# Strided attention tiles in pairs, block 0's logits on VectorE, and another order of the work ahead of the FFN

## The chip, the cores and the metric

The kernel runs on one core of a Trainium2 chip. The metric is the device time of one execution, in microseconds (us).

## What is computed

Attention, a dense FFN and a gated expert layer, one after the other, over 4 x 576 = 2304 tokens of width 512:

```python
mask_local = (rel >= 0) & (rel < 32)
mask_strided = (rel >= 0) & (pos[None, :] % 32 == pos[:, None] % 32)
masks = np.stack([mask_local if h < 4 else mask_strided for h in range(8)])
attn = softmax(where(masks, q @ k.T / 8, -1e9))        # 4 batches, 8 heads of width 64
x = attn @ v                                           # [2304, 512]
...
r = np.maximum(x @ w_in, 0)                            # w_in [512, 2048]
x = (s * r * r + b) @ w_out                            # w_out [2048, 512]
...
skip = x @ w_skip > 0                                  # only these tokens are computed
e = argmax(x @ w_gate)                                 # one of 8 experts
out = x + softmax(x @ w_gate)[e] * (relu(x @ w1[e]) @ w2[e])
```

## The kernel before, in words

**Attention.** The eight heads of a batch are taken as four pairs of heads: two local ones (`loc`, window 32) and two strided ones. The 16 pairs n (batch n // 4) are worked through in the order local, strided, local, strided of each batch, and each is cut into three units g. A local unit has three tiles of 128 queries by 96 keys. A strided unit has 4, 4 and 3 tiles of 108 queries (54 of each head) by 54 keys, since after sorting the positions by their remainder only keys of the same three remainders meet. `add_unit` makes the tasks of a unit: `scores` (PE), `masked` and `top` (DVE), `bias`, `exps` (ACT), `recip`, `norm` (DVE), `turned` (PE: one transpose for each tile, into the PSUM bank `pt`), `moved` (ACT: `pt` to `pts` in SBUF), `mixed` (PE: the products with V, for each tile one matmul for each head, side by side in two column halves of the array), and the puts, `hi` (ACT) and `lo` (DVE), which split the result into two fp32r parts in `xb`, the FFN's input. For pairs from `PAIRED` on the two heads' scores too are computed side by side in column halves of the array; below it they come from one matmul over both heads. For pairs below `BYPE` the mask is added by PE.

**FFN.** There are 6 blocks of 384 tokens and 16 chunks `fc` of the hidden width, so 96 steps i. A step is `mm1` (12 matmuls, L1150), the elementwise `relu`, `square`, `g_hi`, `g_lo`, and `mm2` (9 matmuls, L1193) into three PSUM banks. The first 8 steps are half of block 0, then comes all of block 1, then block 0's second half, then blocks 2 to 5. Block 0 and 1 need batches 0 and 1, the later blocks batches 2 and 3, whose attention units stand between the FFN's steps. The weights come as fp32 and are split into two fp32r parts on DVE and ACT (the last step of a split is L580 on DVE); the eighth pair of weights is wanted at about 100 us, the last one at about 140 us.

**Routing and experts.** When a block is done its logits are computed, on PE (`logits_pe`: four times three transposes, L652, and two matmuls, L666, then a small turn, L681) or on DVE (`logits_v`: 27 dot products, L703, over gate rows that a DMA spreads over all partitions). `DOTS` names the blocks that take DVE. `route_rank` follows, on PE. The experts' phase runs at the end, in its own loops.

**What sets the order.** A planner (`plan.add`) holds every task with its engine costs, its priority, what it waits for and which buffers it takes. It fixes the program order of each engine ahead of time from these costs and from tables of offsets (`UNIT_AT`, `LOAD_AT`, `CHUNK_AT`); on the chip each engine then runs its own list in order and waits on semaphores. DMAs are issued from SP's list.

Of the kernel before, what the change touches and what calls it, by code (L numbers as in the profile page):

```python
# [21 lines left out]
BLK = 384  # L22
# [9 lines left out]
BYPE, SQ_A = 8, 8  # L32
# [4 lines left out]
LATE, LEAD = 3.0, 0  # L37


PAIRED, AHEAD = 8, 2  # L40
TURN_AT, PACE = (26.0, 44.0), 1.4
DOTS = (2, 3)
# [12 lines left out]
    1.1, 1.9, -0.6, -2.9, -0.4, 1.2, -0.7, 12.3, 11.2, -14.2, -8.5, 1.8,  # L55
# [6 lines left out]
]  # L62

SEM, PELAT, DMA, FLEX = 0.34, 0.22, 2.0, 0.4
# [125 lines left out]
def kernel(  # L190
# [53 lines left out]
    sx = [pm.tile([128, 512], F32, name=f"sx{i}") for i in range(2)]  # L244
# [42 lines left out]
    vb = wp.tile([96, 2 * 11 * D], F32, name="vl")  # L287
# [4 lines left out]
    x_tasks = {k: [] for k in range(NBLK)}  # L292
# [14 lines left out]
    def place(n, g):  # L307
        return wanted(n, g) if n < PAIRED else in_turn[3 * (n - PAIRED) + g]

    def add_pair(n):  # L310
# [22 lines left out]
        def load_v(e):  # L333
            if n in V_ROOM:
                for h in range(2):
                    vt[h] = make(vbuf[h], [nk, nt_all, D], F32)
                    SY.dma_start(vt[h][:], vd[:, h])
            else:
                v = vb[0:nk, 0:2 * nt_all * D].rearrange("p (h t d) -> p h t d", h=2, t=nt_all)
                SY.dma_start(v, vd)  # L340
                vt[:] = [v[:, 0], v[:, 1]]
# [17 lines left out]
        if n in V_ROOM:  # L359
            vbuf = [Buf([r]) for r in V_ROOM[n]]  # L360
        lv = plan.add(c_dma(4 * nk * 2 * nt_all * D), load_v, p0 - 3.5 + LOAD_AT[n], after=() if n in V_ROOM else o_tasks.get(n - 1, ()), take=vbuf, lat=DMA)
        s_tasks[n], o_tasks[n] = [], []
        for g in range(3):
            prio = place(n, g)
            add_unit(n, b, hp, g, loc, qk, vt, vbuf, qbuf, nq, nk, by_pe, prio, lq[min(g, 1)], lv)

    def add_unit(n, b, hp, g, loc, qk, vt, vbuf, qbuf, nq, nk, by_pe, prio, lq, lv):
        ts = [3 * g + t for t in range(3)] if loc else [4 * g + t for t in range((4, 4, 3)[g])]
# [7 lines left out]
        xo_b = Buf(["xo0", "xo1"] + ["x2p1", "x2p2"] * first)  # L376
# [50 lines left out]
        def norm(e):  # L427
            ENG[e].tensor_tensor(m3(d["s"]), m3(d["s"]), d["sm"][0:np_, 4:4 + nt, None].to_broadcast([np_, nt, nk]), op=ALU.mult)

        def turned(e):  # L430
            d["pt"] = pt = make(pt_b, [128, 512], F32)
            for i in range(nt):
                PE.transpose(pt[0:nk, i * np_:(i + 1) * np_], m3(d["s"])[:, i, :], ident[0:np_, 0:np_])  # L433

        def moved(e):
            d["pts"] = make(pts_b, [128, 432], F32)
            dst, src = d["pts"][0:nk, 0:nt * nq], d["pt"][0:nk, 0:nt * np_]
            if np_ > nq:
                dst = dst.rearrange("p (t h c) -> p t h c", t=nt, h=2)
                lo = src.rearrange("p (t c) -> p t c", t=nt)  # L440
                src = bass.AP(lo.tensor, lo.offset, [lo.ap[0], lo.ap[1], [64, 2], [1, nq // 2]])
            copy(e, dst, src)

        def cols(i, t):
            lo = 18 if not loc and t == 10 else 0
            return lo, nq // 2 - lo

        def mixed(e):
            d["xo"] = xo = make(xo_b, [128, 512], F32)
            c = 0  # L450
# [14 lines left out]
        if halved and len(mixes) >= AHEAD:  # L465
            t = plan.extend(mixes[-AHEAD], {"PE": nt * (0.16 if loc else 0.12)}, scores, after=[lq], take=[sc_b], use=qbuf)
# [4 lines left out]
        if halved and len(mixes) >= AHEAD:  # L471
            gates.append((turns[-AHEAD], b, prio))
        if not by_pe:
            t = plan.add(c_v(w), masked, prio, after=[t, consts], take=[s_b], use=[sc_b])
        t = plan.add(c_v(w), top, prio, after=[t], take=[sm_b], use=[sc_b] if by_pe else [s_b])
        t = plan.add(c_v(8), bias, prio, after=[t], use=[sm_b])
        t = plan.add({"A": nt * (0.25 + nk / 1400)}, exps, prio, after=[t], take=[s_b] if by_pe else [], use=[sm_b] + ([sc_b] if by_pe else [s_b]))
# [13 lines left out]
        if loc:  # L491
            k_, o = divmod(b * S + 192 * g, BLK)
            parts.append((k_, 192, lambda w_, k_=k_, o=o: xb[k_ % 3][:, w_, hp, o:o + 192], lambda xo: xo[:, 0:192]))
        else:
            r0, nr = 12 * g, n_out // 18
            j0 = 0
            while j0 < 18:
                k_, o = divmod(b * S + 32 * j0, BLK)
                nj = min(18 - j0, (BLK - o) // 32)
                parts.append((k_, nr * nj,  # L500
                              lambda w_, k_=k_, o=o, nj=nj: xb[k_ % 3][:, w_, hp, o:o + 32 * nj].rearrange("p (j r) -> p r j", r=32)[:, r0:r0 + nr, :],
                              lambda xo, j0=j0, nj=nj: xo[:, 0:18 * nr].rearrange("p (r j) -> p r j", j=18)[:, :, j0:j0 + nj]))
# [16 lines left out]
    for n in range(len(pairs)):  # L519
# [863 lines left out]
```

## Time and profile before

| | |
|---|---|
| median of three runs | 743.59 us (741.44 to 744.49) |
| the profiled execution | 741.3 us, its span 739.5 us |
| PE busy | 723.3 us, 98% of the span |
| DVE / ACT / POOL busy | 400.1 / 294.1 / 62.7 us |
| mean granted TensorE clock | 0.992 |
| DMA | 98 GB/s over the span |

The span is the time between the first and the last instruction of the trace; what lies around it (1.8 us) is in the execution's time alone. Matmuls are pipelined and overlap in the trace: what a group of them costs is read from the start of one group to the start of the next, not from its length.

### The profile page before, as it was taken

How to read it: one execution, taken by the hardware profiler on the slowest of the kernel's cores; microseconds unless marked ns; L12 is line 12 of the kernel's file. 1: busy time of each engine (PE TensorE's matmuls, PEld its weight loads, DVE VectorE, ACT ScalarE, POOL GpSimd, SP SyncE). 2: the span in 40 equal slices, each digit the busy share in tenths (PEclk: the TensorE clock that was granted, in tenths of full speed). 3: DMA queues.
4: the chain of work that ended last, by engine and by line, in shares of the span. 5: the costliest groups of instructions: out<-in, count | busy, mean ns of one | idle time of the engine just before them, and what ended most of it. 6: DMA issues, size and time to landing. Idle time of an engine off the chain costs nothing.

```text
span 739.5 us, 12203 instructions
## 1 busy us (share of the span) xinstructions
PE 723.3 (98%) x4513; PEld 623.0 (84%) x4517; DVE 400.1 (54%) x1092; ACT 294.1 (40%) x819; POOL 62.7 (8%) x67
## 2 busy tenths in 40 slices
PE   8899999999999999999999999999999999999996
PEld 6788788998888888888899988898787888888894
DVE  4889999826554744688646664654442222312221
ACT  4777776524353554544422224443211312203120
POOL 0000000000010100000100012110023212122131
PEclk9989999999999999999999999999999999999998
DMA  9875655202240222331021104420203701112021
GB/s 291 279 249 174 205 185 183 85 1 86 92 151 1 74 82 71 132 117 47 30 95 47 45 14 156 154 64 0 86 9 110 291 29 43 44 43 71 30 76 45
DMA packets 26895, 73.74 MB, mean 100 GB/s; under 512 B 5557, under 2 KB 5813, under 8 KB 26821
## 3 DMA queue, kind: packets, MB, share of 16 engines
q1 hardware_dynamic: 22741, 61.56, 25.3%
q0 software_dynamic: 3936, 11.03, 4.7%
q8 instruction: 41, 0.67, 0.4%
q10 hardware_dynamic: 144, 0.22, 0.1%
q14 instruction: 33, 0.27, 0.1%
HBM read 57.67 MB, written 15.13 MB: 98 GB/s over the span
## 4 chain that ended last, share of the span: by engine, by line
PE 81%; issue 5%; DVE 5%; DMA 4%; ACT 3%; POOL 1%; SPq 0%; POOLq 0%; ACTq 0%; DVEq 0%
PE h L1150 25%; PE x2p L1193 24%; PE h L920 10%; PE x2p L933 8%; DMA out<-row,ids 4%; PE sx L455 2%; PE pt L433 2%; PE sx L399 2%; PE sx L401 1%; PE h L1303 1%; DVE xb L462 1%; DMA wo<-in_w_out 1%; PE x2p L985 1%; PE sx L666 1%; PE pt L652 1%
## 5 line engine op out<-in xcount | busy, mean ns | idle before, releaser
L1150 PE MATMUL h<-xb,wi 128*128 128x384 f32 x1152 | 222.8, 342 | 0.5 <-ACT r L1155 0.5
L1150 PEld LDWEIGHTS h<-xb,wi 128*128 128x128 f32 x1152 | 203.4, 188 | 7.8 <-ACT r L1155 0.9
L1193 PE MATMUL x2p<-wo,gh 128*128 128x512 f32 x564 | 194.6, 399 | 0.0
L1193 PEld LDWEIGHTS x2p<-wo,gh 128*128 128x128 f32 x564 | 105.9, 188 | 21.1
L1193 PE MATMUL x2p<-wo,gl 128*128 128x512 f32 x282 | 110.8, 393 | 0.0
L920 PE MATMUL h<-xb,wi 128*128 128x512 f32 (+1 forms) x480 | 103.3, 374 | 1.4 <-DVE row L937 1.0
L920 PEld LDWEIGHTS h<-xb,wi 128*128 128x128 f32 x480 | 83.5, 188 | 19.4 <-issue 1.6
L933 PE MATMUL x2p<-wi,wo 128*128 128x512 f32 x432 | 99.4, 390 | 0.0
L1155 ACT ACTIVATE r<-h 128x384 f32<-128x384 f32 x96 | 47.0, 490 | 128.6 <-PE h L1150 112.6
L1158 DVE SCALAR_TENSOR_TENSOR r<-r,sbc 128x384 f32<-128x384 f32 x88 | 54.3, 617 | 76.6 <-ACT r L1155 76.4
L933 PEld LDWEIGHTS x2p<-wi,wo 128*128 128x128 f32 x432 | 80.7, 188 | 16.6
L923 ACT ACTIVATE wo<-h 128x512 fp32r<-128x512 f32 (+1 forms) x40 | 22.2, 555 | 142.8 <-PE h L920 136.8
L1162 ACT ACTIVATE gh<-r,sbc 128x384 fp32r<-128x384 f32 x88 | 54.3, 617 | 53.0 <-DVE r L1158 30.1
L1167 DVE SCALAR_TENSOR_TENSOR gl<-r,sbc,gh 128x384 fp32r<-128x384 f32 x88 | 54.3, 617 | 33.1 <-ACT gh L1162 27.1
L924 DVE SCALAR_TENSOR_TENSOR wo<-h,wo 128x512 fp32r<-128x512 f32 (+1 forms) x40 | 25.5, 638 | 75.4 <-ACT wo L923 74.4
L822 POOL DMA_INDIRECT lst<-pay,ii x18 | 18.4, 1022 | 496.3 <-DVE ii L816 474.5
L1193 PEld LDWEIGHTS x2p<-wo,gl 128*128 128x128 f32 x282 | 53.1, 188 | 8.0
L937 DVE SCALAR_TENSOR_TENSOR row<-x2p,ids,xb 128x512 f32<-128x512 f32 x14 | 10.5, 750 | 61.7 <-PE x2p L933 61.7
L703 DVE SCALAR_TENSOR_TENSOR junk<-row,lo 128x512 int8<-128x512 f32 x54 | 37.2, 690 | 6.2 <-DMA lo<-wgt 5.3
L462 DVE TENSOR_TENSOR xb<-sx,xb 128x192 fp32r<-128x192 f32 (+4 forms) x64 | 19.6, 333 | 7.8 <-ACT xb L277 5.1
L277 ACT CAST xb<-sx 128x192 fp32r<-128x192 f32 (+4 forms) x56 | 15.9, 337 | 18.0 <-PE sx L401 6.6
L938 POOL DMA_INDIRECT out<-row,ids x14 | 14.0, 997 | 106.1 <-DVE row L937 92.7
(481 smaller groups left out, 769.1 us busy)
## 6 DMA issues: line engine op xcount, KB each, us to landing
wo<-in_w SPq DMA_DIRECT2D x16, 512.0 KB
wo<-in_w_out SPq DMA_DIRECT2D x12, 512.0 KB
x2d<-row SPq DMA_DIRECT2D x21, 256.0 KB
qks<-in_qkstr SPq DMA_DIRECT2D x6, 882.0 KB
wo<-in_w_in SPq DMA_DIRECT2D x10, 512.0 KB
out<-row SPq DMA_DIRECT2D x18, 256.0 KB
lo<-wgt SPq DMA_DIRECT2D x18, 256.0 KB
qkl<-in_qkloc SPq DMA_DIRECT2D x5, 864.0 KB
```

What stands on the lines that cost most here:

```text
L462: V.tensor_tensor(dst(1), src(d["xo"]), dst(0).bitcast(F32), op=ALU.subtract)
L703: V.scalar_tensor_tensor(junk[:], d["rows"][t][:], 1.0, wd["w"][:], op0=ALU.mult, op1=ALU.mult, accum_out=d["lg"][:, t, x:x + 1])
L920: PE.matmul(p[:, 0:N], W[f][:, w, k * 128:(k + 1) * 128], x[:, k, 0:N], start=n == 0, stop=n == 11)
L923: A.activation(h[:, 0, 0:N], p[:, 0:N], AF.Relu)
L924: V.scalar_tensor_tensor(h[:, 1, 0:N], p[:, 0:N], 0.0, h[:, 0, 0:N].bitcast(F32), op0=ALU.max, op1=ALU.subtract)
L933: PE.matmul(y[:], K["h"][f][:, g, c], W[NFE + f][:, w, :], start=n == 0, stop=n == 3 * NFE - 1)
L1150: PE.matmul(p[:, 0:BLK], win_t[fc][:, w, k * 128:(k + 1) * 128], x[:, k, :], start=n == 0, stop=n == 11)
L1155: A.activation(d["r"][:], d["p"][:, 0:BLK], AF.Relu)
L1158: V.scalar_tensor_tensor(d["r"][:], d["r"][:], sbc[:, 0:1], d["r"][:], op0=ALU.mult, op1=ALU.mult)
L1162: A.activation(gh[:], d["r"][:], AF.Identity, bias=sbc[:, 1:2])
L1167: V.scalar_tensor_tensor(gl[:], d["r"][:], sbc[:, 1:2], gt[i][0][:].bitcast(F32), op0=ALU.add, op1=ALU.subtract)
L1193: PE.matmul(x2p[t][:], g[:, c], wout_t[fc][:, w, :], start=begins and n == 0, stop=ends and n == 2)
```

## The change

1. *Strided tiles in pairs.* A strided unit's tiles are now t and t + 6 beside t + 1 and t + 7. The two tiles of a pair stand 64 columns apart in the tile `s_`, so that one transpose of 118 columns turns both: the first to partitions 0 to 53, the second to 64 to 117. The ten columns between them are zeroed by a GpSimd memset for each unit (`gap`). `moved` copies half the columns. V is loaded in two halves, tiles 0 to 5 on partitions 0 to 53 and 6 to 10 on 64 to 117 (two DMAs instead of one). `mixed` then has four matmuls for a pair of tiles, one in each quarter of the array, and the two row halves write to two PSUM banks: `xo0` and `xo1` in batches 0 and 1, `xo` and the end of `pt` in batches 2 and 3. The puts of strided units become twice as many and half as wide, except in batch 1 (g below 2), where one instruction reads both banks.
2. *`PAIRED` 8 to 4.* Batch 1's scores are computed in column halves too; their mask is still added by PE, now by two matmuls.
3. *`EARLY` = 4.* The first four `mm1` are cut into 9 matmuls that need the first three pairs of heads (`x_first`) and 3 matmuls (`mm1_last`) that need the fourth.
4. *`DOTS` with block 0.* Its logits go from PE to DVE.
5. *Order.* Batch 1's units have a hand-written order (`SECOND`), the tables and a few planner constants change, and the squares of steps 8 and 9 go the way of the first eight (`SQ_A` 8 to 10).

```diff
-PAIRED, AHEAD = 8, 2
+LATE, LEAD = 3.3, 0
+
+
+PAIRED, AHEAD = 4, 2
...
+SECOND, SECOND_AT = (0, 4, 3, 5, 11, 6, 9, 10, 1, 2, 7, 8), (-5.11, 0.99)
...
-DOTS = (2, 3)
+DOTS = (0, 2, 3)
+EARLY = 4
...
         def load_v(e):
-            if n in V_ROOM:
+            if not loc:
+                v = make(vbuf[0], [128, 2, 6, D], F32)[:] if n in V_ROOM else vb[:, 0:12 * D].rearrange("p (h t d) -> p h t d", h=2, t=6)
+                vt[:] = [v[:, h] for h in range(2)]
+                for r, t in ((0, slice(0, 6)), (1, slice(6, 11))):
+                    SY.dma_start(v[64 * r:64 * r + nk, :, 0:t.stop - t.start].rearrange("p h t d -> p h (t d)"), vd[:, :, t].rearrange("p h t d -> p h (t d)"))
...
+        ts = [3 * g + t for t in range(3)] if loc else [2 * g + t for t in ((0, 6, 1, 7), (0, 6, 1, 7), (0, 6, 1))[g]]
...
+        xo_b = [Buf(["xo0", "xo1"] + ["x2p1", "x2p2"] * first)]
+        if not loc:
+            xo_b = [Buf([f"xo{r}"] + [f"x2p{r + 1}"] * first) for r in range(2)] if b < 2 else [*xo_b, pt_b]
...
+            if by_pe and halved:
+                for h in range(2):
+                    PE.matmul(m3(sc)[64 * h:64 * h + nq // 2], idb[0:np_, 64 * h:64 * h + nq // 2], mask, start=True, stop=False)
+            elif by_pe:
                 PE.matmul(m3(sc), idb[0:nq, 0:nq], mask, start=True, stop=False)
...
+        def gap(e):
+            d["s"] = make(s_b, [128, 288], F32)
+            G.memset(d["s"][0:np_, 0:256].rearrange("p (t k) -> p t k", k=128)[:, :, 54:64 if nt == 4 else 118], 0.0)
...
         def turned(e):
             d["pt"] = pt = make(pt_b, [128, 512], F32)
-            for i in range(nt):
-                PE.transpose(pt[0:nk, i * np_:(i + 1) * np_], m3(d["s"])[:, i, :], ident[0:np_, 0:np_])
+            if loc:
+                for i in range(nt):
+                    PE.transpose(pt[0:nk, i * nq:(i + 1) * nq], s3(d["s"])[:, i, :], ident)
+            else:
+                for i in range(0, nt, 2):
+                    PE.transpose(pt[0:118, i // 2 * np_:(i // 2 + 1) * np_], d["s"][0:np_, 64 * i:64 * i + 118], ident[0:np_, 0:np_])
 
         def moved(e):
-            d["pts"] = make(pts_b, [128, 432], F32)
-            dst, src = d["pts"][0:nk, 0:nt * nq], d["pt"][0:nk, 0:nt * np_]
-            if np_ > nq:
-                dst = dst.rearrange("p (t h c) -> p t h c", t=nt, h=2)
-                lo = src.rearrange("p (t c) -> p t c", t=nt)
-                src = bass.AP(lo.tensor, lo.offset, [lo.ap[0], lo.ap[1], [64, 2], [1, nq // 2]])
-            copy(e, dst, src)
-
-        def cols(i, t):
-            lo = 18 if not loc and t == 10 else 0
-            return lo, nq // 2 - lo
+            d["pts"] = make(pts_b, [128, 384], F32)
+            k, c = (nk, nt * nq) if loc else (118, np2 * np_)
+            copy(e, d["pts"][0:k, 0:c], d["pt"][0:k, 0:c])
...
+            d["xo"] = [d["pt"][:, 384:512] if x is pt_b else make(x, [128, 512], F32) for x in xo_b]
...
+                r, j = i % 2, i // 2
+                lo = 18 if t == 10 else 0
...
+                    c = j * np_ + h * (np_ - 54)
+                    PE.matmul(d["xo"][r][64 * h:64 * h + 64, 54 * j:54 * (j + 1) - lo], vt[h][64 * r:64 * r + 54, 2 * g + j, :], d["pts"][64 * r:64 * r + 54, c + lo:c + 54], start=True, stop=True)
...
+            both = b == 1 and g < 2
+            for r in range(1 if both else 2):
+                r0, nr = 30 if g == 2 and r else 18 * r + 6 * g, 2 if g == 2 and r else 6
...
+    def products(p, X, L, fc, ks, begins, ends):
+        todo = [(k, w, x) for k in ks for w, x in ((0, X), (0, L), (1, X))]
+        for n, (k, w, x) in enumerate(todo):
+            PE.matmul(p[:, 0:BLK], win_t[fc][:, w, k * 128:(k + 1) * 128], x[:, k, :], start=begins and n == 0, stop=ends and n == len(todo) - 1)
...
+            products(p, X, L, fc, HPS[0:3] if i < EARLY else range(4), True, i >= EARLY)
+
+        def mm1_last(e, d=d, blk=blk, fc=fc):
+            products(d["p"], xb[blk % 3][:, 0], xb[blk % 3][:, 1], fc, HPS[3:], False, True)
...
+        if i < EARLY:
+            m1 = plan.add(c_pe(BLK, 9, False), mm1, i - 3000, after=x_first + w_done["i", fc], take=[h_b], use=[wbuf["i", fc]])
+            m1 = plan.add(c_pe(BLK, 3, False), mm1_last, i - 3000, after=[m1, *after, *x_tasks[0]], use=[h_b, wbuf["i", fc]])
```

In the rows below, `x12` counts equal instructions behind one another, `im` is the identity, `s__` a unit's probabilities, `qks`, `qkl` and `vl` the loaded queries, keys and values, `wi_` and `wo_` weights or what shares their buffers.

**A strided unit among the FFN's steps.** PE's list in block 4's attention, before: a transpose for each of four tiles, an `mm1`, the eight products in one bank, the next unit's scores, its transposes.

```order
L433 MATMUL pt<-im,s__3489 54x118 x4
L1150 MATMUL h<-xb_88,wi_876 128x384 x12
L455 MATMUL sx_91<-pts,vl 64x54 x8
L399 MATMUL sx_92<-qks 54x54 x6
L433 MATMUL pt<-im,s__3584 54x118 x4
```

After, at block 2's units: two transposes of 118 rows, an `mm1`, the products in fours, each four with two in bank `sx` and two in bank `pt`.

```order
L461 MATMUL pt<-im,s__2515 118x118 x2
L1181 MATMUL h<-xb_90,wi_696 128x384 x12
L480 MATMUL sx<-pts,vl 64x54 x2
L480 MATMUL pt<-pts,vl 64x54 x2
L480 MATMUL sx<-pts,vl 64x54 x2
L480 MATMUL pt<-pts,vl 64x54 x2
L416 MATMUL sx<-qks 54x54 x6
```

What moved: two of four transposes are gone, and neighbouring products now lie in different row halves; their number is the same.

**The first FFN steps.** PE's list before, around the first `mm1` (L1150; L1146 are matmuls that only keep the clock up): the 12 matmuls stand together, behind the last unit of block 0.

```order
L1146 LDWEIGHTS im
L1146 MATMUL h<-im 128x512
L1150 MATMUL h<-xb_88,wi_530 128x384 x12
L455 MATMUL sx_92<-pts,wi_596 64x64
L455 MATMUL sx_92<-pts,wo_598 64x64
L455 MATMUL sx_92<-pts,wi_596 64x64
L455 MATMUL sx_92<-pts,wo_598 64x64
L455 MATMUL sx_92<-pts,wi_596 64x64
L455 MATMUL sx_92<-pts,wo_598 64x64
L433 MATMUL pt<-im,s__641 96x128 x3
```

After, at the second `mm1` (the nine matmuls with `wi_518` of the first stand 19 rows further up):

```order
L1195 MATMUL h<-im 128x512
L1181 MATMUL h<-xb_88,wi_696 128x384 x9
L1181 MATMUL h<-xb_88,wi_518 128x384 x3
L458 MATMUL pt<-im,s__707 96x128 x3
L473 MATMUL x2p_756<-pts,wi_245 64x64
L473 MATMUL x2p_756<-pts,wo_247 64x64
L473 MATMUL x2p_756<-pts,wi_245 64x64
L473 MATMUL x2p_756<-pts,wo_247 64x64
L473 MATMUL x2p_756<-pts,wi_245 64x64
L473 MATMUL x2p_756<-pts,wo_247 64x64
L1181 MATMUL h<-xb_88,wi_696 128x384 x3
```

What moved: nine matmuls each of the first two steps stand ahead of the last strided unit's puts, and three of each behind them, with a local unit of batch 1 between.

**Block 0's logits.** PE's list before, one of four rounds of three transposes and two matmuls between the parts of the FFN's steps.

```order
L666 MATMUL sx_91<-pts,wgr 18x384
L666 MATMUL sx_91<-lo,wgr 9x384
L652 MATMUL pt<-im,row 128x128 x3
L1150 MATMUL h<-xb_90,wi_1012 128x384 x12
L666 MATMUL sx_91<-pts,wgr 18x384
```

After, PE's list has no such rows for block 0; the work is in DVE's list, between the FFN's elementwise steps (L1206 `square`, L1215 `g_lo`) and the next units' (L427 `masked`, L431 `top`, L434 `bias`, L486 put).

```order
L1206 SCALAR_TENSOR_TENSOR r<-r,sbc 128x384
L1215 SCALAR_TENSOR_TENSOR gl<-r,sbc,gh 128x384
L1206 SCALAR_TENSOR_TENSOR r<-r,sbc 128x384
L427 TENSOR_TENSOR s__2974<-sx,im 128x288
L486 TENSOR_TENSOR xb_88<-sx,xb_88 128x192
L431 TENSOR_REDUCE sm<-s__2974 128x3
L747 SCALAR_TENSOR_TENSOR junk,lg<-row,lo 128x512
L1215 SCALAR_TENSOR_TENSOR gl<-r,sbc,gh 128x384
L747 SCALAR_TENSOR_TENSOR junk,lg<-row,lo 128x512 x2
L434 TENSOR_SCALAR sm<-sm 128x3
```

What moved: 27 dot products (L747) stand in DVE's list across twelve steps, and block 0's `route_rank` on PE, which waits for the last of them, stands some ten steps later than before.

## Rows read from the trace of the kernel before

**Rows 1.** The page's chain that ended last, shares of the span by engine.

```profile
PE 81%; issue 5%; DVE 5%; DMA 4%; ACT 3%; POOL 1%; SPq 0%; POOLq 0%; ACTq 0%; DVEq 0%
```

**Rows 2.** Stretches: busy PE, PEld, DVE, ACT, POOL (instructions), clock, DMA share, GB/s.

```profile
24.00:42.00 18.00, 15.65 (x177) 13.66 (x176) 15.13 (x58) 12.79 (x57) 0.00 (x0) 0.82 0.74 232
42.00:101.00 59.00, 56.61 (x463) 48.57 (x465) 54.55 (x154) 46.29 (x155) 0.00 (x0) 1.00 0.63 200
101.00:140.00 39.00, 38.51 (x194) 34.73 (x193) 38.43 (x72) 24.98 (x45) 0.00 (x0) 1.00 0.57 182
140.00:515.00 375.00, 374.96 (x2448) 330.88 (x2447) 218.48 (x624) 154.37 (x421) 20.99 (x20) 1.00 0.22 72
```

**Rows 3.** Timeline of PE: start, length, line, operation; strided units of batches 2 and 3.

```profile
235.09 0.57 PE L433 MATMUL pt<-im,s__2547 118*54 118x118 f32 x4
235.42 0.48 PE L1193 MATMUL x2p<-wo,gh 128*128 128x512 f32 x1
...
237.95 0.67 PE L455 MATMUL sx<-pts,vl 54*64 54x54 f32 x16
238.56 0.39 PE L399 MATMUL sx<-qkl 128*64 128x96 f32 x4
...
241.74 0.54 PE L455 MATMUL sx<-pts,vl 54*64 54x54 f32 x12
242.22 0.47 PE L399 MATMUL sx<-qkl 128*64 128x96 f32 x6
```

**Rows 4.** Timeline of PE, single matmuls of two strided units of batch 1.

```profile
72.01 0.22 PE L455 MATMUL sx<-pts,wi 54*64 54x54 f32 x1
72.02 0.22 PE L455 MATMUL sx<-pts,wo 54*64 54x54 f32 x1
72.07 0.22 PE L455 MATMUL sx<-pts,wi 54*64 54x54 f32 x1
...
87.67 0.20 PE L455 MATMUL sx<-pts,wi 54*64 54x36 f32 x1
87.67 0.20 PE L455 MATMUL sx<-pts,wo 54*64 54x36 f32 x1
87.70 0.22 PE L455 MATMUL sx<-pts,wi 54*64 54x36 f32 x1
```

**Rows 5.** Timeline of PE, logits of block 0.

```profile
222.23 0.34 PE L666 MATMUL sx<-pts,wgr 128*18 128x384 f32 x1
...
222.58 0.49 PE L652 MATMUL pt<-im,row 128*128 128x128 f32 x3
222.83 0.42 PE L1150 MATMUL h<-xb,wi 128*128 128x384 f32 x1
...
237.67 0.36 PE L681 MATMUL pt<-im,lo 18*128 18x18 f32 x3
```

**Rows 6.** Dots on DVE: the page's row of L703, and the stretch of block 2's.

```profile
L703 DVE SCALAR_TENSOR_TENSOR junk<-row,lo 128x512 int8<-128x512 f32 x54 | 37.2, 690 | 6.2 <-DMA lo<-wgt 5.3
...
246.00:300.00 54.00, 53.96 (x448) 46.53 (x448) 28.18 (x88) 27.66 (x99) 2.63 (x3) 1.00 0.21 70
300.00:352.00 52.00, 52.00 (x420) 45.45 (x418) 41.26 (x124) 24.74 (x79) 0.00 (x0) 1.00 0.34 106
```

**Rows 7.** Waits of DVE from 20 to 101: us, times, longest.

```profile
DVE xb L462 <- ACT xb L277: 3.8, 5, 1.3
```

**Rows 8.** The put on DVE by width, busy and mean ns.

```profile
L462 DVE TENSOR_TENSOR xb<-sx,xb 128x144 fp32r<-128x144 f32 x15 | 6.2, 412 | 3.7 <-ACT xb L277 2.3 <-ACT s__1134 L419 1.3
...
L462 DVE TENSOR_TENSOR xb<-sx,xb 128x72 fp32r<-128x72 f32 x15 | 4.2, 283 | 1.5 <-ACT s__886 L419 0.8 <-ACT xb L277 0.6
```

**Rows 9.** Timelines around 100: DVE's end of a weight, PE's start with it.

```profile
99.44 0.69 DVE L580 TENSOR_TENSOR wo<-row,wo 128x512 fp32r<-128x512 f32 x1
...
101.46 0.40 PE L1193 MATMUL x2p<-wo,gh 128*128 128x512 f32 x1
```

**Rows 10.** The chain of waits, 36 to 45: start, length.

```profile
42.31 2.15 PE h L1150 x12
```

More of the change, by code (lines that the diff above doesn't have):

```diff
@@ L54 @@
 LOAD_AT = [
[L55 removed]
+    2.1, 2.4, -0.9, -2.7, -1.0, 1.2, -2.6, 12.3, -14.2, 6.8, -8.5, 1.8,
     1.6, -9.2, 4.2, 0.7,
@@ L241 @@
     xb = [wp.tile([128, 2, 4, BLK], F32R, name=f"xb{i}") for i in range(3)]
-    sx = [pm.tile([128, 512], F32, name=f"sx{i}") for i in range(2)]
+    sxs = pm.tile([128, 2, 512], F32, name="sx")
+    sx = [sxs[:, i] for i in range(2)]
     halves = {f"sc{i}": sx[i][:, 0:SCW] for i in range(2)} | {f"xo{i}": sx[i][:, SCW:512] for i in range(2)}
@@ L286 @@
     qks = wp.tile([128, S + 2 * 11 * 54], F32, name="qks")
-    vb = wp.tile([96, 2 * 11 * D], F32, name="vl")
+    vb = wp.tile([128, 2 * 9 * D], F32, name="vl")
     HPS = (0, 2, 1, 3)
@@ L291 @@
     PER_B = 12
-    x_tasks = {k: [] for k in range(NBLK)}
+    x_tasks, x_first = {k: [] for k in range(NBLK)}, []
     s_tasks, o_tasks, last_qk, early = {}, {}, {}, []
@@ L451, in mixed @@
+        def mixed(e):
+            d["xo"] = [d["pt"][:, 384:512] if x is pt_b else make(x, [128, 512], F32) for x in xo_b]
+            if loc:
+                for i, t in enumerate(ts):
+                    for h in range(2):
+                        PE.matmul(d["xo"][0][64 * h:64 * h + 64, 64 * i:64 * i + 64], vt[h][:, t, :], d["pts"][0:nk, i * nq + 64 * h:i * nq + 64 * h + 64], start=True, stop=True)
+                return
             for i, t in enumerate(ts):
-                lo, m = cols(i, t)
+                r, j = i % 2, i // 2
+                lo = 18 if t == 10 else 0
@@ L465, in add_unit @@
         if halved and len(mixes) >= AHEAD:
-            t = plan.extend(mixes[-AHEAD], {"PE": nt * (0.16 if loc else 0.12)}, scores, after=[lq], take=[sc_b], use=qbuf)
+            t = plan.extend(mixes[-AHEAD], {"PE": nt * (0.17 if loc else 0.1) + by_pe * w / 2200}, scores, after=[lq], take=[sc_b], use=qbuf)
         else:
@@ L507, in add_unit @@
+        for k_, m, x_b, dst, src in parts:
+            hi = plan.add({**c_a(m, True), **c_v(m)}, lambda e, dst=dst, src=src: put(e, 0, dst, src), prio, after=[t], use=x_b)
+            lo = plan.add(c_v(m), lambda e, dst=dst, src=src: put(e, 1, dst, src), prio, after=[hi], use=x_b)
             x_tasks[k_] += [hi, lo]
+            if k_ == 0 and n < 3:
+                x_first.extend([hi, lo])
     def small_loads(e):
@@ L517 @@
     consts = plan.add({"SP": 0.4}, small_loads, -2, lat=DMA)
-    for n in range(len(pairs)):
-        add_pair(n)
+    for n in (*range(4), *range(8, len(pairs))):
+        if n == 8:
+            units = [u for k in range(4, 8) for u in add_pair(k)]
+            for k in SECOND:
+                units[k]()
+            mixes.clear()
+            turns.clear()
+        for u in add_pair(n):
+            u()
     fill_b = Buf(["row"])
@@ L1007, in last_x2 @@
         ls = sp.tile([128, BLK], F32, name="r", bufs=1)
-        lt = pm.tile([128, 512], F32, name="sx1")
+        lt = sx[1]
         for t in range(3):
@@ L1042, in experts @@
         fill(3)
-        rk, cn = (pm.tile([128, 512], F32, name=n_) for n_ in ("sx0", "sx1"))
+        rk, cn = sx
         route_rank(NBLK - 1, rk)
```

107 lines of the change are left out of this document (52 added, 55 removed), and 8 rows, old and new, of tables (CHUNK_AT, UNIT_AT).

## Prediction

> **What bounds the kernel now.** I read the page first: the chain that ended last is 81% PE [rows 1]. Then a table of stretches, to see where PE is really the limit [rows 2]. From 140 to 515 PE is busy 374.96 of 375 us and DVE 218.48: whatever PE is spared there comes off the time, and DVE has room. From 101 to 140 DVE is busy 38.43 of 39, and from 42 to 101 54.55 of 59, with PE at 56.61: ahead of 140 DVE, which splits the weights, sets the pace, and PE follows closely behind. The weights' timelines say the same: DVE starts the last step of the eighth output weight at 99.44 for 0.69, and PE's matmul with it starts at 101.46 [rows 9], 1.3 us later. So there are two kernels here: a head up to about 140 in which DVE's list counts, and a long part behind it in which only PE's does. From 24 to 42 neither is full (15.65 and 15.13 of 18) and the granted clock is 0.82 on average, so in part of it the lower level of 1.2 GHz [rows 2].
>
> **Batches 2 and 3, transposes.** These 12 strided units (8 of four tiles, 4 of three) stand in the full stretch. Four transposes take 0.33 from their start to the next group's (235.09 to 235.42) [rows 3], 0.083 each; the change drops 2, 2 and 1 of each pair's 4, 4 and 3. That is 4 pairs x 5 x 0.083 = 1.7 us. That the new ones turn 118 rows instead of 54 I price at nothing: the logits' transposes of 128 x 128, three in 0.25 (222.58 to 222.83) [rows 5], are no slower than these.
>
> **The same units' products.** The sixteen matmuls of a four-tile unit (each product is two passes) take 0.61 (237.95 to 238.56), the twelve of a three-tile unit 0.48 (241.74 to 242.22) [rows 3]. The single starts show how: the two column halves start 0.01 apart, and the next two 0.06 after the first [rows 4]. So eight pairs stand 0.06 apart, and what is over is start and end. In quarters four matmuls could share each 0.06: four groups instead of eight save 4 x 0.06 = 0.24, and in a three-tile unit, whose last tile has no partner, 2 x 0.06 = 0.12. That gives 8 x 0.24 + 4 x 0.12 = 2.4 us. No row of this trace shows two row halves at work together, so it is bounded: 0 (they take turns) to 2.4. I take 2.4, since the two column halves, the nearest case, do overlap almost fully. Against this change speaks a rule of the Trainium skill, TensorEngine Tiling (Array Packing), section Instruction Overhead: each matmul has some 60 cycles of overhead, so no tiling factor should come out of a dimension that is already small, and 54 columns are below it. At 2.4 GHz it would be 25 ns each, an estimate from that page: sixteen of them at 0.40 against eight pairs at 0.48, a gain of 0.08 a unit, under 1 us in all. The trace disagrees with it as a floor: two matmuls of 36 columns start together at 87.67 and the next at 87.70 [rows 4].
>
> **Block 0's logits.** They leave PE in the full stretch. A pair of logit matmuls takes 0.35 (222.23 to 222.58), three transposes 0.25 (222.58 to 222.83), four times each; the last turn 0.28 (237.67 [rows 5] to 237.95 [rows 3]). That is 4 x 0.60 + 0.28 = 2.7 us. DVE gets 27 dots of 0.69 [rows 6], 18.6 us over the twelve steps on which they stand. Its load in 246 to 300, about as long and with attention units, is 28.18 of 54; with the dots it would be 46.8, 87%. In 300 to 352, where block 2's dots ran, it was 41.26 of 52, 79%, and PE stayed at 52.00 of 52 [rows 6]: this is the work that hides them. They also wait for the gate rows from DMA, 5.3 us for two blocks [rows 6], so up to 2.7 more for block 0, which would bring DVE to 92%. What is queued behind such a wait is `square` and `g_lo`, and PE's `mm2` waits for these. I put nothing for it in this sum, and up to 2.7 in the bound. `route_rank` of block 0 stands some ten steps later, so its wait should be over when PE comes to it.
>
> **The head.** PE is spared more here (column halves for batch 1's scores, fewer transposes), but that is no gain where DVE sets the pace. DVE's list changes in two ways. Sixteen strided puts come on top (12 in batch 0, 4 in batch 1): two of 72 columns are 2 x 0.283 against 0.412 for one of 144 [rows 8], 0.15 each, 2.5 us at most. Ahead of the eighth weight some local units have moved behind it, which about balances this; up to the last weight it is up to 2.3 more. I take 0.7, because puts overlap their neighbours. On the other side is DVE's idle time: 2.9 us from 24 to 42 and 4.5 from 42 to 101 [rows 2], of which 3.8 (20 to 101) are puts that wait for the copy on ACT before them [rows 7]. That is where the new order acts: the first nine matmuls of the first four steps no longer wait for the fourth pair of heads, behind which the first step's twelve now run from 42.31 for 2.15 us [rows 10], and batch 1's units are dealt out by hand. I take four fifths of the 3.8, 3.1 us. The head then gives 3.1 - 0.7 = 2.4. Bounds: all 7.4 of idle time gone and no more work, -7.4; nothing gone and all the work paid, +2.3.
>
> **New waits.** Batches 2 and 3 now have four puts instead of two on DVE for a strided unit, and the last unit's stand right ahead of blocks' first `mm1`; nine of twelve matmuls (2.15 x 9 / 12 = 1.6 us [rows 10]) cover a chain of four puts of 0.28 [rows 8] behind their copies. The bank `pt` is held until the puts are done, so the next transposes come later. I put 0.5 for both, bounds 0 and 1.5. The memsets are GpSimd's, which is idle there, and the second V DMA is early enough to hide behind a unit's scores.
>
> **The sum.** -1.7 - 2.4 - 2.7 - 2.4 + 0.5 = -8.7 us on the profiled execution's 741.3 us, so 732.6 there. The median of the runs, 743.59, is 2.3 above that execution, so I forecast 743.6 - 8.7 = 734.9 for the median.
>
> **The rivals.** Half a per cent, 3.7 us, is about what a measurement of this kernel can tell from no change.
> (a) *The head gives nothing or loses.* DVE is 98.5% busy from 101 to 140, and a put added there delays every weight behind it. With the head between 0 and +2.3 the sum is -6.3 to -4.0: 737.3 to 739.6. For it speaks that DVE's list grows, against it the idle time up to 101. Chance 0.2.
> (b) *The quarters don't overlap.* Row halves take turns, the products save nothing: -8.7 + 2.4 = -6.3, 737.3. The overhead rule above comes near it, at -8.7 + 1.5 = -7.2, 736.4. No row shows row halves, so 0.12.
> (c) *The other side: PE waits for DVE in block 0's logits.* The dots stand among `square` and `g_lo`, and DVE's spare time there is some 13%, 7 us of 54, less 2.7 for the gate rows. It decides if the attention units of batch 2 make these twelve steps uneven: wherever DVE has more work than time for a few steps on end, PE's `mm2` stands, and every us of it is lost, since PE has no other slack. Gains elsewhere are 8.7, so it must cost over 12 us to be measurably slower, about two thirds of the dots' 18.6 unhidden. Block 2's dots speak against it. Time 744 to 751. Chance 0.06.
> (d) *It doesn't do what it says.* The order puts new waits into the head that cost what the late part gains (6.8): PE then idles more from 24 to 42, where its clock has already fallen, and the lower level stretches what follows. 740 to 745. Chance 0.08.
>
> **Numbers.** The forecast (sum -6 to -13) has the remaining 0.54, with 731 to 738. The range takes in (a) and (b), and the lower bound where all idle time of the head goes: 728 to 741. About one and a half in ten lies outside, mostly above. Faster by over 0.5% (below 739.9): the forecast, (b), and nearly all of (a), 0.84. Within 0.5%: the rest of (a) and most of (d), 0.10. Slower: (c), 0.06.
>
> **What the profile would show.** Two transposes in about 0.17 and products of a four-tile unit in about 0.37 from start to next start; if these stay at 0.6, (b) holds. No matmuls of the logits between 215 and 240, PE still full there, DVE at 85 to 92%; a PE wait on `g_lo` there is (c). The last weights ready some 2 us earlier than before; if the eighth weight's step ends at 99 or later, (a) holds. What would make the forecast wrong by more than its range is a wait of PE that the present trace has no place for, above all on the banks `pt` and `xo` or on the row buffers that block 0's dots hold for twelve steps.

## The result and the profile after

The changed kernel takes 752.21 us (752.05 to 752.59), the kernel before 743.88 in the same comparison: a ratio of 1.0119, 95% interval 1.0096 to 1.0142. It is slower by 8.3 us; 734.9 was forecast. The profiled execution has a span of 750.3 us. From the page, its span and PE's busy time:

```profile
span 750.3 us, 12497 instructions
...
PE 719.2 (96%) x4545; PEld 613.6 (82%) x4546; DVE 420.2 (56%) x1199; ACT 291.6 (39%) x837; POOL 67.9 (9%) x92
```

PE is busy for less time than before, 719.2 us against 723.3, and yet the span is 10.8 us longer: PE stands idle for 31.1 us against 16.2. Where, the stretches of [rows 2] say, here of the changed kernel, in the same columns:

```profile
24.00:42.00 18.00, 15.38 (x124) 12.80 (x125) 13.18 (x62) 9.25 (x42) 0.37 (x3) 0.53 0.45 153
42.00:101.00 59.00, 51.16 (x512) 41.10 (x511) 54.28 (x160) 44.02 (x149) 1.11 (x6) 0.97 0.62 206
101.00:140.00 39.00, 39.00 (x247) 34.46 (x243) 38.28 (x84) 27.51 (x63) 0.00 (x0) 1.00 0.60 192
140.00:515.00 375.00, 374.91 (x2436) 330.17 (x2435) 241.65 (x712) 156.40 (x445) 24.45 (x33) 1.00 0.24 80
```

From 140 to 515 PE is as full as before. From 24 to 101 it is idle for 10.5 us (4.7 before), and from 24 to 42 its granted clock is 0.53 on average (0.82 before). A finer cut is the time at which fixed points of the program are reached. Step 30's `mm2` stands behind the head and ahead of block 0's logits, step 95's is the last. "Head" is how much later than before the first is reached, "late part" what is lost or won from there to the second, "behind it" the same from the second to the end of the span (us, from rounded times, so that a part can be off by 0.1; the experiments' kernels, e1 to e9, follow below). Each row is one execution: the one of the kernel before took 741.3 us, 1.8 to 2.6 under the medians of its runs up to e7, and that of e9 (742.09) is the longest of its ten. The kernel before had a median of 743.13 beside e1 to e4, 743.82 beside e5 to e7 and 742.00 beside e8 and e9, so a difference of medians across these groups is uncertain by about 1 us.

| kernel (profiled execution) | head | late part | behind it | span |
|---|---|---|---|---|
| before: step 30 at 204.4, step 95 at 517.0 | | | | 739.5 |
| after | +7.2 | -6.2 | +9.8 | 750.3 |
| *experiments* | | | | |
| e1, two tiles | +0.2 | -5.9 | +0.8 | 734.6 |
| e2, only the turns' third tile elsewhere | +7.0 | -5.4 | +2.9 | 744.1 |
| e3, before with one tile | +9.7 | +0.6 | +9.0 | 758.9 |
| e4, two tiles, logits on PE | -0.2 | -1.6 | +0.8 | 738.5 |
| e5, two tiles, more PE work in the head | +1.3 | -3.4 | +0.6 | 738.0 |
| e6, two tiles, more DVE work in the head | +4.1 | -4.9 | +0.6 | 739.3 |
| e7, two tiles, `EARLY` = 0 | +3.3 | -5.6 | +1.0 | 738.2 |
| e8, two tiles, tables of before | +13.4 | -6.2 | +0.7 | 747.4 |
| e9, two tiles, `FLEX` = 0.4 | +4.8 | -5.0 | +0.9 | 740.3 |

The late part, on which most of the forecast was spent, came out as forecast: -6.2 against -6.3 (-1.7 - 2.4 - 2.7 + 0.5). Its operations in the changed kernel, from PE's timeline in the columns of [rows 3]:

```profile
226.66 0.36 PE L461 MATMUL pt<-im,s__2610 118*118 118x118 f32 x2
226.79 0.48 PE L1241 MATMUL x2p<-wo,gh 128*128 128x512 f32 x1
...
229.04 0.27 PE L480 MATMUL sx<-pts,vl 54*64 54x54 f32 x2
229.06 0.27 PE L480 MATMUL pt<-pts,vl 54*64 54x54 f32 x2
229.14 0.23 PE L480 MATMUL sx<-pts,vl 54*64 54x54 f32 x2
229.16 0.22 PE L480 MATMUL pt<-pts,vl 54*64 54x54 f32 x2
229.20 0.22 PE L480 MATMUL sx<-pts,vl 54*64 54x54 f32 x2
...
229.43 0.55 PE L416 MATMUL sx<-qkl 128*64 128x96 f32 x8
```

The two transposes (L461) take 0.13 to the next group's start, the sixteen product matmuls (L480) 0.39 (229.04 to 229.43; 0.38 in the median of the eight units), where [rows 3] had 0.33 and 0.61. The starts show why: four matmuls, two into bank `sx` and two into bank `pt`, now start within 0.02 us, and the next four start 0.10 after the first, those behind them 0.06 later. The quarters do work at once.

The head was forecast to win 2.4 and lost 7.2, and 9.8 us appeared in the experts' phase, which the prediction did not speak of at all. PE's waits there (us in all, times, longest):

```profile
PE sx L939 <- DVE xb L946: 6.9, 4, 1.8
...
PE sx L1045 <- ACT row L280: 0.7, 1, 0.7
```

Before, no wait of PE for the tile `sx` was there. One of the four, in the timeline of all engines (what stands in brackets is the idle time before the row and what ended it):

```profile
564.62 0.60 PE L939 MATMUL pt<-im,qkl 128*128 128x128 f32 x4
...
565.06 0.60 PE L939 MATMUL sx<-im,qkl 128*128 128x128 f32 x4
565.26 0.59 ACT L942 CAST xb<-pt 128x512 fp32r<-128x512 f32 x1 [16.21 <-PE pt L939]
565.74 0.59 ACT L942 CAST xb<-sx 128x512 fp32r<-128x512 f32 x1
565.87 0.69 DVE L946 TENSOR_TENSOR xb<-pt,xb 128x512 fp32r<-128x512 f32 x1 [0.25 <-ACT xb L942]
...
566.48 0.68 DVE L946 TENSOR_TENSOR xb<-sx,xb 128x512 fp32r<-128x512 f32 x1
567.22 0.66 PE L939 MATMUL sx<-im,qks 128*128 128x128 f32 x4 [1.56 <-DVE xb L946]
```

L939 are the transposes of an expert's gathered rows, in four groups into four banks: `pt`, the two halves of `sx`, `h`. The third group, into the second half of `sx`, starts only when DVE has read the first half (L946, 566.48 to 567.16). In the kernel before the three groups stand 0.43 apart:

```profile
562.95 0.60 PE L895 MATMUL pt<-im,qkl 128*128 128x128 f32 x4
563.38 0.60 PE L895 MATMUL sx<-im,qkl 128*128 128x128 f32 x4
563.82 0.60 PE L895 MATMUL sx<-im,qks 128*128 128x128 f32 x4
```

What differs is in a part of the diff that I had left out as a matter of names:

```diff
-    sx = [pm.tile([128, 512], F32, name=f"sx{i}") for i in range(2)]
+    sxs = pm.tile([128, 2, 512], F32, name="sx")
+    sx = [sxs[:, i] for i in range(2)]
...
-                pt = pm.tile([128, 4, 128], F32, name=("pt", "sx0", "sx1")[t])
+                pt = sx[t - 1].rearrange("p (k c) -> p k c", k=4) if t else pm.tile([128, 4, 128], F32, name="pt")
```

The two banks were two tiles and are now one tile, so that one instruction of batch 1's puts can read both. If the program's waits are put in by tile, each access to one bank now waits for the other bank's; the experiments try that.

### The profile page after: what moved, and what is told of

It reads as the page before. It is cut to its first block, busy times and chain, and to the rows that moved or that the text cites. A ratio compares the mean times of both kernels' runs of the same rounds, so it can differ in the third digit from the quotient of the medians.

```text
span 750.3 us, 12497 instructions
## 1 busy us (share of the span) xinstructions
PE 719.2 (96%) x4545; PEld 613.6 (82%) x4546; DVE 420.2 (56%) x1199; ACT 291.6 (39%) x837; POOL 67.9 (9%) x92
## 4 chain that ended last, share of the span: by engine, by line
PE 80%; DVE 7%; issue 5%; DMA 4%; ACT 3%; POOL 1%; DVEq 0%; POOLq 0%; ACTq 0%
PE h L1181 25%; PE x2p L1241 24%; PE h L964 11%; PE x2p L977 9%; DMA out<-row,ids 4%; PE sx L416 2%; PE sx L473 1%; PE sx L480 1%; DVE xb L486 1%; PE pt L458 1%; ACT gh L441 1%; PE h L1356 1%; PE sx L418 1%; DVE sm L431 1%; PE x2p L1029 1%
## 5 line engine op out<-in xcount | busy, mean ns | idle before, releaser
L1206 DVE SCALAR_TENSOR_TENSOR r<-r,sbc 128x384 f32<-128x384 f32 x86 | 52.9, 615 | 43.9 <-ACT r L1203 43.7
L1215 DVE SCALAR_TENSOR_TENSOR gl<-r,sbc,gh 128x384 fp32r<-128x384 f32 x86 | 52.9, 615 | 38.0 <-ACT gh L1210 37.0
L747 DVE SCALAR_TENSOR_TENSOR junk<-row,lo 128x512 int8<-128x512 f32 x81 | 55.8, 689 | 18.5 <-DMA lo<-wgt 17.3
L981 DVE SCALAR_TENSOR_TENSOR row<-x2p,ids,xb 128x512 f32<-128x512 f32 x14 | 10.5, 751 | 63.5 <-PE x2p L977 63.5
L280 ACT CAST xb<-sx 128x72 fp32r<-128x72 f32 (+5 forms) x60 | 14.3, 282 | 26.3 <-PE sx L416 15.0
L982 POOL DMA_INDIRECT out<-row,ids x14 | 13.9, 995 | 112.6 <-DVE row L981 99.3
L486 DVE TENSOR_TENSOR xb<-sx,xb 128x72 fp32r<-128x72 f32 (+5 forms) x73 | 18.1, 281 | 4.8 <-ACT s__671 L441 1.4
```

What stands on the lines that cost most here:

```text
L486: V.tensor_tensor(dst(1), src(d["xo"]), dst(0).bitcast(F32), op=ALU.subtract)
L747: V.scalar_tensor_tensor(junk[:], d["rows"][t][:], 1.0, wd["w"][:], op0=ALU.mult, op1=ALU.mult, accum_out=d["lg"][:, t, x:x + 1])
L1206: V.scalar_tensor_tensor(d["r"][:], d["r"][:], sbc[:, 0:1], d["r"][:], op0=ALU.mult, op1=ALU.mult)
L1215: V.scalar_tensor_tensor(gl[:], d["r"][:], sbc[:, 1:2], gt[i][0][:].bitcast(F32), op0=ALU.add, op1=ALU.subtract)
```

## The experiments

**The two banks as two tiles again.** The merged puts of batch 1 become two instructions within the same task, so the planned order stays.

```diff
-    sxs = pm.tile([128, 2, 512], F32, name="sx")
-    sx = [sxs[:, i] for i in range(2)]
+    sx = [pm.tile([128, 512], F32, name=f"sx{i}") for i in range(2)]
...
-                pt = sx[t - 1].rearrange("p (k c) -> p k c", k=4) if t else pm.tile([128, 4, 128], F32, name="pt")
+                pt = pm.tile([128, 4, 128], F32, name=("pt", "sx0", "sx1")[t])
```

> The changed kernel, but the two PSUM banks sx are two tiles again, as before the change; the merged puts of batch 1 become two instructions in the same task, so the planned order stays. Theory A (one tile over two banks makes the work on one bank wait for the other bank's readers and writers, in the attention units as in the experts' turns): the four waits of PE of 1.6 to 1.8 us in the experts' phase go (752.2 - 7 = 745 from these alone), and the head, whose step 20 starts 7.3 us later than before, loses most of that too: 733 to 739 in all. Theory B (the head is late because of the new order and DVE's longer list, the experts' phase because of the shared tile): only the experts' part comes back, 743 to 746.

Measured: 736.55 us (736.31 to 737.12), ratio to before 0.9906 (0.9882 to 0.9929). Theory A holds, and this version beats both kernels: 15.7 us less than the changed one, 9.0 of them behind step 95 and 7.0 in the head. How the head lost them shows at 24 us. In the changed kernel a put of DVE (L486) runs from 24.25, and PE's next matmuls into `sx` (L403) wait for it; the windows of 4 us then have the granted clock in the third column from the right:

```profile
24.25 0.53 DVE L486 TENSOR_TENSOR xb<-sx,xb 128x36 fp32r<-128x36 f32 x3 [0.84 <-ACT gh L441]
...
24.84 0.93 PE L403 MATMUL sx<-im 128*128 128x224 bf16 x4 [1.38 <-DVE xb L486]
```

```profile
20.00:24.00 4.00, 3.27 (x52) 2.85 (x49) 2.11 (x10) 3.08 (x17) 0.00 (x0) 1.00 0.98 378
24.00:28.00 4.00, 3.16 (x20) 2.69 (x24) 2.24 (x15) 1.51 (x5) 0.00 (x0) 0.58 0.82 302
28.00:32.00 4.00, 3.50 (x39) 3.21 (x41) 1.70 (x5) 1.49 (x8) 0.21 (x1) 0.50 0.74 229
32.00:36.00 4.00, 2.97 (x28) 2.20 (x24) 3.90 (x16) 3.28 (x18) 0.16 (x2) 0.50 0.07 26
36.00:40.00 4.00, 3.75 (x43) 2.80 (x42) 3.34 (x17) 2.80 (x13) 0.00 (x0) 0.50 0.10 31
40.00:44.00 4.00, 4.00 (x56) 3.67 (x56) 3.56 (x14) 0.76 (x3) 0.11 (x1) 0.79 0.73 211
```

PE's busy time falls to 3.27 and 3.16 of 4, and from 24 on the granted clock is at its lower level of 1.2 GHz (0.50) until past 40, so that each wait is followed by matmuls that take twice as long; DVE and ACT, which wait for these, are below 2.3 of 4 from 24 to 32. With two tiles the same matmuls (L402 there) start at 23.07, ahead of the same put at 23.24, and the granted clock is 1.00 until 28 and 0.97 to 32; it falls only at the end of that window, and for less time:

```profile
23.07 0.56 PE L402 MATMUL sx<-im 128*128 128x224 bf16 x4
...
23.24 0.41 DVE L487 TENSOR_TENSOR xb<-sx,xb 128x72 fp32r<-128x72 f32 x2 [0.70 <-ACT gh L440]
```

```profile
20.00:24.00 4.00, 3.92 (x60) 3.58 (x58) 2.57 (x15) 3.38 (x18) 0.00 (x0) 1.00 1.02 339
24.00:28.00 4.00, 3.73 (x55) 3.11 (x54) 4.00 (x22) 2.58 (x12) 0.37 (x3) 1.00 0.88 329
28.00:32.00 4.00, 2.12 (x42) 1.70 (x42) 4.00 (x16) 4.00 (x24) 0.00 (x0) 0.97 0.70 215
32.00:36.00 4.00, 3.67 (x25) 3.25 (x25) 4.00 (x23) 1.64 (x5) 0.00 (x0) 0.60 0.74 237
...
42.00:101.00 59.00, 52.50 (x476) 42.60 (x476) 57.00 (x170) 46.37 (x158) 1.24 (x5) 0.97 0.61 202
101.00:140.00 39.00, 39.00 (x238) 34.83 (x237) 38.83 (x78) 26.30 (x55) 0.00 (x0) 1.00 0.55 173
```

The whole head, up to step 30's `mm2`, in the same columns: the kernel before, the first run's (two tiles) and the changed one.

```profile
0.00:204.40 204.40, 196.63 (x1424) 170.92 (x1428) 153.05 (x418) 121.04 (x380) 2.61 (x8) 0.98 0.51 166
0.00:204.62 204.62, 191.99 (x1494) 163.79 (x1500) 156.35 (x458) 120.21 (x389) 4.81 (x21) 0.98 0.51 165
0.00:211.64 211.64, 197.75 (x1498) 167.94 (x1500) 156.22 (x448) 120.39 (x382) 4.15 (x21) 0.95 0.48 160
```

With one tile instead of two PE is idle for 13.9 us instead of 12.6 there, and busy for 197.75 instead of 191.99. So only 1.3 of the 7.0 us is waiting; the other 5.8 is the same list of PE taking longer, and the granted clock from 24 to 42 is 0.53 there and 0.91 with two tiles. Against the kernel before, two tiles spare PE 4.6 us, and it idles 4.9 longer: that is the head's +0.2.

**Only the experts' turns.** The changed kernel, but the third group's transposes go to bank `h`.

```diff
-                pt = sx[t - 1].rearrange("p (k c) -> p k c", k=4) if t else pm.tile([128, 4, 128], F32, name="pt")
+                pt = pm.tile([128, 4, 128], F32, name="pt") if t == 0 else sx[0].rearrange("p (k c) -> p k c", k=4) if t == 1 else ph.tile([128, 4, 128], F32, name="h")
```

> The changed kernel, but in the experts' turns the third tile's transposes go to the second buffer of bank h, not to the second half of the shared tile. Theory A and B alike: the four waits of PE for the put of the other half (6.9 us in the trace) go, the head stays 7.3 us late: 744 to 746. A rival, that the experts' phase is long for another reason (its token lists or its weights come later): 751 to 753.

Measured: 746.05 us (744.27 to 747.72), 6.2 less than the changed kernel, the head unchanged at +7.0. So the four waits cost what the trace said, 6.9, and are apart from the head's loss. Of the 9.8 behind step 95, 2.9 are left; the first run left 0.8, so 2.1 more hang on the tile elsewhere, in block 5's own turns (L1045) at least, 0.7 in the waits above.

**The kernel before with one tile.** Nothing else is changed: no pairs, no dots, the old order.

```diff
-    sx = [pm.tile([128, 512], F32, name=f"sx{i}") for i in range(2)]
+    sxs = pm.tile([128, 2, 512], F32, name="sx")
+    sx = [sxs[:, i] for i in range(2)]
```

> The kernel before, with nothing changed but that its two banks sx become one tile of two banks, as in the changed kernel. Theory A: the experts' phase gains four or five waits of some 1.7 us (+7) and the attention units' work waits across banks, in the head above all: 743.6 + 7 + 3 to 10 = 753 to 761. Theory B: +7 only, 750 to 752. If the tracking is by bank after all: 743 to 745.

Measured: 760.65 us (760.2 to 760.76), ratio 1.0225 (1.0201 to 1.025): +17.5 us from the tile alone; in the traces, which are 19.4 apart, 9.7 of it lies in the head and 9.0 behind step 95. Its waits of PE, first from 18 to 101, then from 515 on:

```profile
PE sx L456 <- DVE xb L463: 2.3, 2, 2.0
PE sx L456 <- DVE sm L423: 1.5, 1, 1.5
PE sx L393 <- DVE xb L463: 1.3, 2, 1.1
PE sx L456 <- ACT s__640 L420: 1.2, 1, 1.2
...
PE sx L896 <- DVE xb L903: 6.9, 4, 1.8
```

The last row is the changed kernel's wait to the digit, 6.9 us in four of up to 1.8, with none of the change's other parts present. In this kernel's head most of the loss is waiting: up to step 30 PE is idle for 15.8 us (7.8 before) and busy for 198.3 (196.6).

**Block 0's logits back on PE, with two tiles** (`DOTS = (2, 3)`).

> The first run's kernel (two tiles), with block 0's logits on PE again. What DVE's dots save PE is 2.7 us by the rows of before, if no new wait eats it: 2 to 3 us longer than the first run. If the dots make PE wait for DVE, the same or shorter.

Measured: 740.55 us (740.29 to 743.0), 4.0 more than the first run; in the traces the late part is 4.3 longer. From start to next start, the logits' matmuls, transposes and turns take 5.4 us between step 30 and step 95 there and 2.7 in the first run, so the operations cost the 2.7 that was forecast. The 1.6 above it is waiting in another planned order: 0.7 behind one unit's transposes, whose products wait for ACT (0.44, to 290.21), 1.3 among the `mm2` (0.49 of it for `g_lo`, to 352.59), 0.3 in `route_rank`, less 0.7 among the `mm1`. So in that kernel only 1.6 of the 4.2 us that transposes and products save by their rows arrive.

**What sets the head with two tiles.** Its first `mm1` starts at 33.5 instead of 41.8 us, and yet it wins nothing (+0.2). Two runs add work to one engine in the same order: three matmuls more ahead of each `mm1` of steps 4 to 9 (`KEEP_N` 4 to 10), or one addition of 128x384 on DVE in each of the first ten steps.

```diff
-WARM, KEEP_S, KEEP_M, KEEP_N = 18, 4, 3, 4
+WARM, KEEP_S, KEEP_M, KEEP_N = 18, 4, 3, 10
```

> The two-tile kernel with three idle-keeping matmuls (128x512, whose result the next matmul overwrites) put ahead of mm1 in steps 4 to 9 too: 18 more on PE, some 4 us of PE work between 65 and 100 us, in the same order. If DVE's list sets the pace of the head (DVE 57.0 of 59 us busy from 42 to 101 there, PE 52.5), the time grows by less than 1.5 us: 736 to 738. If PE sets it, by about 4: 740 to 741.

```diff
             V.tensor_scalar(d["r"][:], d["r"][:], sbc[:, 0:1], sbc[:, 1:2], op0=ALU.mult, op1=ALU.add)
+            V.tensor_tensor(spare[:], im[:, 0:384], im[:, 0:384], op=ALU.add)
```

> The two-tile kernel with one more addition of 128x384 on DVE, into a tile that nobody reads, in each of the first ten steps: 10 x 0.5 = 5 us more in DVE's list ahead of about 105 us, in the same order. If DVE's list sets the pace of the head, 4 to 5.5 us longer: 740.5 to 742. If PE or ACT sets it, under 2 us: 736.5 to 738.5.

Measured: 739.54 us (738.34 to 742.99) and 740.75 us (739.92 to 743.44). By the table, PE's 4.1 us (7.0 us of L1196's busy time against 2.9) cost the head 1.1 and DVE's 5.6 us cost it 3.9. So DVE bounds the head more than PE does, but not hard: seven tenths of its extra work came through, and a quarter of PE's. The whole time of the DVE run is the forecast one; that of the PE run lies between its two expectations. Work added to ACT alone was not tried. In the profile of the first run the head's waits of PE are for DVE and for ACT, small and many; the three longest from 42 to 105:

```profile
PE pt L457 <- DVE sm L443: 1.9, 1, 1.9
PE sx L479 <- ACT pts L279: 1.4, 1, 1.4
PE pt L460 <- DVE s__1234 L449: 1.1, 1, 1.1
```

The rest of the PE run's loss, 2.5 us, is not in the head: it arises from step 48 to 62, where nothing was changed. PE's waits from 140 to 515 of that run:

```profile
PE sx L849 <- DVE xb L487: 1.0, 1, 1.0
PE sx L472 <- DVE mx L804: 0.9, 1, 0.9
PE x2p L1242 <- DVE gl L1216: 0.5, 1, 0.5
```

L849 is block 0's `route_rank`, and all three wait for DVE. The first two end at 300.26 and 296.00, right behind the last of block 0's dots (295.1); the third, at 362.00, stands behind block 2's dots too, and the kernel with block 0's logits on PE has the like of it (0.49, to 352.59), so it isn't theirs. In the first run only the first of these waits is there, 0.6 us. That a head shifted by 1.1 us makes the dots late is argued from these rows, no run isolates it.

**The early start.** `EARLY = 0`, the first four `mm1` whole, with two tiles.

> The two-tile kernel with EARLY = 0: the first four mm1 whole again, behind the fourth pair of heads. If the head is bound by DVE's list from 42 us on, the first step, now 8 us ahead of before, starts later and little is lost: 736 to 738.5. If the early start is worth what it looks like, 5 to 8 us longer: 741 to 745.

Measured: 740.83 us (739.09 to 742.57), 4.3 more, between the two expectations. In the head 3.1 of it are lost, a little over half of the 5.8 us by which the first `mm1` starts later (39.26 against 33.50).

**The order.** Two tiles with the tables, `FLEX`, `LATE` and `SQ_A` of before, and batch 1's units without the hand-written list; and two tiles with `FLEX = 0.4` alone.

> The two-tile kernel with the order's numbers of before: UNIT_AT, LOAD_AT, CHUNK_AT, LATE, FLEX and SQ_A of before, and batch 1's units by UNIT_AT instead of the hand-written list. The late part's saving (some 6 us) is made of operations and should stay. If the head gives nothing because DVE's work is what it is, the order matters little: 735 to 739. If the new order is what keeps the head from losing (more puts, the same weights), 740 to 746.

> The two-tile kernel with FLEX = 0.4 as before: the planner gives a copy that ACT or DVE can do less readily to DVE. If DVE's list sets the head's pace, a shorter list is worth something, if ACT (46 of 59 us busy there) takes it without new waits: 733 to 737. If the tables fit one value of FLEX only, 738 to 744.

Measured: 750.92 us (749.18 to 753.74) and 739.17 us (735.57 to 742.09). The order matters more than either expectation said: with the old tables the late part still wins 6.2, but the head loses 13.4. From 42 to 101 and 101 to 140 of that kernel:

```profile
42.00:101.00 59.00, 49.14 (x440) 38.85 (x440) 55.81 (x155) 45.79 (x146) 0.88 (x6) 0.97 0.64 205
101.00:140.00 39.00, 32.89 (x199) 29.56 (x200) 36.52 (x83) 25.60 (x65) 0.00 (x0) 0.82 0.52 167
```

DVE is idle for 3.2 and 2.5 us, PE for 9.9 and 6.1, and the granted clock is 0.82 from 101 to 140, where it was 1.00. With `FLEX` alone the ratio to before is 0.9949 (0.9929 to 0.9969), whose interval just touches the first run's. In its trace the head is 4.6 longer, but that execution is 2.9 above the median of this kernel, so a usual head loses less.

## Why the prediction was wrong

**The step that failed: "New waits".** That term, 0.5 with bounds 0 and 1.5, looked at the puts and the bank `pt` among the late FFN steps. The sum had no term for the two banks becoming one tile, and no rival named it. That is the cause of the wrong sign: the one tile costs 15.7 us in the changed kernel (752.21 - 736.55) and 17.5 in the kernel before, in the head and in the experts' phase. The prediction's last paragraph did say that a wait of PE on `pt` and `xo` would put the time out of its range (`xo0` and `xo1` are the ends of the two `sx` banks), but gave it no price and no chance. With two tiles the kernel takes 736.55 us, inside the range and 1.6 above the forecast; it wins 6.6 us on the kernel before where 8.7 was forecast, and 4.9 in the traces, so that it comes so near is in part luck with the executions. I had read the lines as a renaming and compared what each instruction does, not what it waits for.

**Late part: right.** Transposes: 8 x (0.33 - 0.13) + 4 x (0.23 - 0.13) = 2.0 where I had 1.7; products: 8 x (0.60 - 0.38) + 4 x (0.47 - 0.37) = 2.2 where I had 2.4. The rival that the quarters take turns fell, and with it the reading of the overhead rule in the Trainium skill, TensorEngine Tiling (Array Packing), section Instruction Overhead, as a floor for each matmul: sixteen of them at the estimate's 25 ns would be 0.40 for the starts alone, and the sixteen starts lie within 0.24 us. (The change puts tiles of 54 rows into the row halves; it takes nothing from the 54 columns that the prediction held against it.) The logits' 2.7 are borne out by the fourth run's rows, and the three together give 6.9, of which 6.2 arrived; 0.5 had been set aside for new waits. DVE stayed below the 85 to 92% that were forecast beside the dots: 40.48 of 50 us from 250 to 300, 81%, in the changed kernel.

**Head: the step that failed beside it.** "Four fifths of the 3.8, 3.1 us" of DVE's idle time were to go. With two tiles DVE's idle time from 42 to 101 did fall, from 4.5 to 2.0, and the first `mm1` started 8 us earlier, but the head gave +0.2 and not -2.4: DVE was busy 57.0 of 59 there against 54.6, so what it no longer waited it worked. Up to step 30 its work grew by 3.3 us (156.35 against 153.05), where the sum had 0.7. By the traces that is rival (a), at the end of its range at which the head gives nothing; the median, 736.55, lies just below (a)'s 737.3, and since the traced execution of the kernel before is 1.8 under its median beside e1, a gain of that size in usual executions stays open. That idle time of DVE can be counted as a gain when its list grows too was wrong. That DVE's weights set the pace up to 140 was too wide: the last weight was ready 1.8 us earlier (144.4 against 146.2), as forecast, and nothing came of it, because with two tiles PE's last wait ahead of step 30 ends at 87.5 and it is busy for 39.00 of 39 us from 101 to 140. The last pair of weights is not wanted at about 140 either: step 23 is the first to use it, and its `mm1` starts at 156.7 in the kernel before.

**Rival (d)** named the mechanism by which the head was lost in the changed kernel, waits from 24 to 42 with the clock at its lower level behind them, at a chance of 0.08, but gave no cause for them, and its 740 to 745 had nothing for the experts' phase. **Rival (c)**, block 0's dots, exists in small: 0.6 us of PE's waiting for DVE in the two-tile kernel, 1.9 in the one with more PE work, 0.09 in the changed kernel.

## What to carry to other kernels

A change in how buffers are declared is a change in what waits for what: before a diff of tiles is priced at nothing, list for each instruction on the two buffers what it now waits for. Where PE is full, savings counted from start to next start can arrive nearly whole (6.2 of 6.9 us here), but another order can eat them as waits (1.6 of 4.2 with the logits on PE); where another engine sets the pace, count that engine's list, idle time and added work together. If one instruction must see two banks, its price is every other pair of instructions that used these banks apart.

## What the runs showed of the hardware that was not expected

Matmuls of 54 rows in the four quarters of the array, into two banks, start four within 0.02 us, and the next four 0.10 and then 0.06 later, where two did every 0.06 before: the products of a four-tile unit fell from 0.60 to 0.38 us. And a short wait of PE in the head cost more than itself: 1.4 us of it at 24.84, behind a stretch in which PE was busy 3.27 of 4 us, stands at the start of 20 us at a granted clock of 0.50 to 0.79 (four-us windows), in which pairs of score matmuls start 0.36 apart (L418, 30.21 to 30.57) that start 0.19 apart in the two-tile kernel (L417, 23.70 to 23.89). Over the head that is 5.8 us of longer busy time against 1.3 of longer waiting. That this wait is what lowered the clock is argued from the order of the rows.
